# A retention layer and two feed-forward layers on one core: GpSimd's arithmetic placed on VectorE, and each attention unit issued in two halves around the two products of a step

## The chip, the core and the metric

The kernel runs on one NeuronCore of a Trainium2 chip. A core has TensorE (in profiles PE, and PEld for its weight loads), VectorE (DVE), ScalarE (ACT), GpSimd (POOL) and SyncE (SP), which issues most DMAs. The metric is the device time of one execution in microseconds. The kernel before takes 620.3 us (median of three runs, 618.93 to 621.04).

## The reference

Three layers follow each other, all in fp32. The first is a retention layer over 2 batches, 8 heads, 768 positions and head size 64; the two others are feed-forward layers over 1536 tokens, 512 wide inside and 2048 hidden.

```
state = gamma[h] * state + k_t v_t^T          # per batch, head, position t
y_t   = scale * q_t state
x     = y, tokens x 512
x     = softplus(x @ w1_in) @ w1_out          # written as max(h,0) + log1p(exp(-|h|))
out   = (h * clip(h + 3, 0, 6) / 6) @ w2_out, h = x @ w2_in
```

The weights arrive as float64, so every weight is turned into fp32 on the chip from its two 32-bit words.

## The kernel before

**Attention units.** Each batch is cut into 6 pieces of 128 positions, a *unit* each, 12 in all (u = 0 to 11). A unit takes all 8 heads. `scores` multiplies transposed k and q (32 small matmuls per unit in all parts together), and VectorE multiplies both halves by a mask-and-decay table into `pt`. `prepare(u + 1)` transposes k and q of the next unit on TensorE, ScalarE copies them out of PSUM, and `decayed` multiplies v by a table into `vs` (VectorE for units 0 and 1, GpSimd for the others). `carry` multiplies q by the running state `bd` into `o`, and `fade` then scales `bd` by a decay (two GpSimd instructions of 64 x 256). `intra` adds `vs` times `pt` to `o`; VectorE scales the sum into `on`, ScalarE rounds it into `x_hi` (fp32r), and GpSimd subtracts to get the rest, `x_lo`. `state` multiplies k by `vs` and VectorE adds the product to `bd`.

**Feed-forward steps.** A step s is one hidden block f of 128 for one chunk of 512 tokens. `gemm1` multiplies the two parts of `w_in` by the two parts of x in 12 matmuls of 512 columns; ScalarE and VectorE turn the sum into g by `g`, `e`, and split it into `hi` (ScalarE) and `lo` (VectorE). `gemm2`, two steps later (LAG = 2), multiplies `hi` and `lo` by the parts of `w_out` in 12 more matmuls and adds them up in four PSUM banks that are held for a whole chunk. Steps 0 to 15 need chunk 0 only, so units 4 to 11 run beside steps 0 to 7.

**Weights.** `fetch` loads the raw words; `convert` makes a weight tile: ScalarE scales the upper words, VectorE makes four operations (`raw` clamp, `w` shift, two more `w` combinations), then the tile is split into two parts, `t[:, 0]` and `t[:, 1]`. For the first 8 tiles ScalarE copies and GpSimd subtracts (line 97); for the others ScalarE writes -w into `t[:, 1]`, a DMA issued by GpSimd adds w to it (line 100), and ScalarE copies `t[:, 0]`. All 32 tiles of layer 1 are converted beside steps 0 to 15.

**PSUM.** There are eight banks; `bank()` hands them out in rotation. While a chunk holds four, the other four serve the units and `gemm1`: seven requests in a unit with its step, so the bank of a request was last used by the one four requests earlier, and a matmul waits until that bank has been read out.

**Order.** Every engine works through its queue in order. Until unit 3 the queues follow the program. From then on (`nc.on = False`) a scheduler sorts the instructions by when it thinks that they can run, with their place in the program as priority. Line 148 starts the loop in which unit u is followed by step s.

All instructions are recorded on line 31 of a helper, so the profile's groups are told apart by tile names.

Of the kernel before, what the change touches and what calls it, by code (L numbers as in the profile page):

```python
# [10 lines left out]
F32 = mybir.dt.float32  # L11
# [3 lines left out]
ALU = mybir.AluOpType  # L15
# [26 lines left out]
def kernel(ctx, tc, q, k, v, w1_in, w1_out, w2_in, w2_out, tq, tk, tc_, tg, out):  # L42
    nc = InOrder(tc)
# [11 lines left out]
    LAG = 2  # L55
# [27 lines left out]
    def convert(m, o, f):  # L83

        raw = raws.pop((m, o, f))
        low, y = raw[:, :, 0], raw[:, :, 1]

        w = cv_p.tile([P, CH], U32, tag="w", name="w")
        nc.scalar.activation(y.bitcast(F32), y.bitcast(F32), AF.Copy, scale=2.0 ** -112)
        nc.vector.tensor_scalar(y.bitcast(F32), y.bitcast(F32), -TOP, TOP, ALU.max, ALU.min)  # L90
        nc.vector.tensor_scalar(w, y, 3, None, ALU.logical_shift_left)
        nc.vector.scalar_tensor_tensor(w, y, 0x80000000, w, ALU.bitwise_and, ALU.bitwise_or)
        nc.vector.scalar_tensor_tensor(w, low, 29, w, ALU.logical_shift_right, ALU.bitwise_or)
        t = (wout_p if o else win_p).tile([P, 2, CH], F32R, tag="w", name="w_parts")
        if done[1] < 2 * EARLY:
            nc.scalar.activation(t[:, 0], w.bitcast(F32), AF.Copy)
            nc.gpsimd.tensor_tensor(t[:, 1], w.bitcast(F32), t[:, 0].bitcast(F32), ALU.subtract)
        else:
            nc.scalar.activation(t[:, 1], w.bitcast(F32), AF.Copy, scale=-1.0)
            nc.gpsimd.dma_start(out=t[:, 1].bitcast(F32), in_=w.bitcast(F32), accum_op=ALU.add)  # L100
            nc.scalar.activation(t[:, 0], w.bitcast(F32), AF.Copy)
        if o:
            w_out_t[m, f] = t
        else:
            w_in_t[m, f] = t.rearrange("p a (k n) -> p a k n", k=KD)
# [40 lines left out]
    with ExitStack() as actx:  # L146
        unit = attention(actx, tc, nc, q, k, v, tq, tk, tc_, tg, x_hi, x_lo, CH, bank, feed, fetch_weights)
        for u in range(CH // P, NU):
            unit(u)
            step(s)  # L150
            s += 1
    while s < n_steps:
        step(s)
# [3 lines left out]
def attention(ctx, tc, nc, q, k, v, tq, tk, tcc, tg, x_hi, x_lo, CH, bank, feed, fetch_weights):  # L157
# [43 lines left out]

    def decayed(u):
        vs = wk.tile([P, H, D], F32, tag="vs" + "0" * (u < START), name="vs", bufs=2)
        (nc.vector if u < 2 else nc.gpsimd).tensor_tensor(
            vs, nat["v", u], tk_sb.rearrange("p (h o) -> p h o", o=1).to_broadcast([P, H, D]), ALU.mult)
        tr["vs", u] = vs

# [12 lines left out]
    def carry(u):  # L220
        b, i = units[u]
        qT = tr["q", u]
        o = ps(NP, C)
        tr["o", u] = o
        if i > 0:
            for p in range(NP):
                nc.tensor.matmul(o[:, p, :], bd[b][:, p, :], qT[:, p, :], start=(p == 0), stop=False, skip_group_check=True)
        fade(u)

    def intra(u):  # L230
        b, i = units[u]
        vs, pt, o = tr["vs", u], tr["pt", u], tr["o", u]
        for h in range(H):
            g = h % 2
            nc.tensor.matmul(o[g * D:(g + 1) * D, h // 2, :], vs[:, h, :], pt[:, g, h // 2, :],
                             start=(i == 0 and h < 2), stop=True, skip_group_check=True)
        c, at = divmod(u * C, CH)
        hi, lo = x_hi[c][:, :, at:at + C], x_lo[c][:, :, at:at + C]
        on = wk.tile([P, NP, C], F32, tag="on" + "0" * (u < START), name="on", bufs=2)
        nc.vector.tensor_tensor(on, o, tq_sb, ALU.mult)  # L240
        nc.scalar.activation(hi, on, AF.Copy)
        nc.gpsimd.tensor_tensor(lo, on, hi.bitcast(F32), ALU.subtract)

    def state(u):
        b, i = units[u]
# [15 lines left out]
    def fade(u):  # L261
        b, i = units[u]
        if i == 0 or i == NCH - 1:
            return
        for j in range(2):
            r = slice(j * D, (j + 1) * D)
            s = bd[b][r, :, r]
            nc.gpsimd.tensor_tensor(s, s, tc_sb[r].rearrange("p (n o) -> p n o", o=1).to_broadcast([D, NP, D]), ALU.mult)

    for t in bd:  # L270
        nc.vector.memset(t, 0.0)
# [15 lines left out]
    def prepare(u):  # L287
        transposed(u, "k")
        transposed(u, "q")
        decayed(u)  # L290
# [18 lines left out]
        fetch(u, "k", "q", "v")  # L309

    def unit(u):
        scores(u)
        if u + 3 < len(units):
            fetch(u + 3, "k", "q", "v")
        if u + 1 < len(units):
            prepare(u + 1)
        carry(u)
        intra(u)
        state(u)

    return unit

# [1 line left out]
def moe(ctx, tc, nc, out, x_hi, x_lo, w_in_t, w_out_t, chunks1, chunks2, NF, KD, DM, CH, LAG, feed, first, bank, release):  # L324
# [71 lines left out]

    n1 = len(chunks1)

    def step(s):
        if s < len(steps):  # L400
            m, c, ci, f = steps[s]
            gemm1(m, c, ci, f)
            if m == 0 and ci == 0:
                feed(first(f))
            if m == 0 and ci == n1 - 1:
                feed(2 * NF + f + 1)
            if m == 1 and ci == 0:
                feed(3 * NF + f + 1)
        if LAG <= s < len(steps):
            gemm2(*steps[s - LAG])  # L410
        if s == len(steps):
            gemm2(*steps[s - LAG], *(f for _, _, _, f in steps[s - LAG + 1:]))

    return step, LAG, len(steps) + 1
# [38 lines left out]
```

## Time and profile before

| | us |
|---|---|
| median of three runs | 620.3 |
| the profiled execution's own time | 619.72 |
| its span | 617.9 |
| TensorE busy | 595.0 |
| VectorE busy | 353.6 |
| ScalarE busy | 277.5 |
| GpSimd busy | 102.2 |

The profiled execution is 0.6 us under the median; 1.8 us of it lie outside the span. Busy time of TensorE counts a matmul from issue to its modelled end and consecutive matmuls overlap, so a row that starts when the row in front is still running means an engine without a pause. An idle time in a row of groups is the engine's idle time just before these instructions, and the arrow names what ended it.

### The profile page before, as it was taken

The page shows a single profiled execution, that of the slowest core. Times are in us where ns is not written, and L with a number is a line of the kernel's source. Part 1 is how long each engine was busy: PE and PEld are TensorE (multiplying, and loading weights), DVE is VectorE, ACT ScalarE, POOL GpSimd, SP SyncE. Part 2 cuts the span into 40 slices and gives each one's busy share as a digit, 9 for nine tenths or more (in the row PEclk, how much of TensorE's full clock was granted, in tenths as well). Part 3 has the DMA queues.
Part 4 walks back from the last instruction along what each step waited for, and adds up shares of the span by engine and source line. Part 5 has one row for each costly group of instructions (what it writes and reads, how often), then busy time and mean ns, then how long its engine had stood idle before and what let it go on. Part 6 is the DMA issues. An engine that isn't in the chain of part 4 may idle for free.

```text
span 617.9 us, 7766 instructions
## 1 busy us (share of the span) xinstructions
PE 595.0 (96%) x2963; PEld 489.4 (79%) x2963; DVE 353.6 (57%) x583; ACT 277.5 (45%) x473; POOL 102.2 (17%) x110
## 2 busy tenths in 40 slices
PE   7988787999999999999999999999999999999997
PEld 6866576788888888888877878888888888888886
DVE  4599999899863433366667799822422222322223
ACT  3354556578653333465556678722222222222220
POOL 1755455432100000011111123200000000000000
PEclk9999899999999999999999999999999999999999
DMA  9998877788810000045567789700100000100001
GB/s 194 232 235 229 207 183 188 175 216 209 198 37 1 0 1 1 0 95 128 136 152 188 162 203 256 148 0 1 53 16 0 2 1 0 69 0 1 0 1 68
DMA packets 69511, 61.60 MB, mean 100 GB/s; under 512 B 40033, under 2 KB 56673, under 8 KB 69473
## 3 DMA queue, kind: packets, MB, share of 16 engines
q1 hardware_dynamic: 61408, 46.42, 26.8%
q0 software_dynamic: 8064, 14.68, 14.4%
q8 instruction: 23, 0.38, 0.3%
q14 instruction: 16, 0.12, 0.1%
HBM read 43.26 MB, written 3.15 MB: 75 GB/s over the span
## 4 chain that ended last, share of the span: by engine, by line
PE 73%; DVE 14%; DMA 5%; issue 4%; ACT 3%; SPq 1%; POOL 0%; DVEq 0%; POOLq 0%; ACTq 0%
PE banks L31 73%; DVE w L31 6%; DMA raw<-in_moe_w_in_dram 3%; DVE raw L31 2%; DVE g L31 1%; DVE pt L31 1%; DVE e L31 1%; DMA q<-in_q_dram 1%; DVE lo L31 1%; DMA w_parts<-w 1%; ACT raw L31 1%; DVE bd L31 1%; ACT e L31 1%; ACT hi L31 1%; SPq L31 1%
## 5 line engine op out<-in xcount | busy, mean ns | idle before, releaser
L31 PE MATMUL banks<-x_hi,w_parts 128*128 128x512 f32 x768 | 254.6, 392 | 0.0
L31 PEld LDWEIGHTS banks<-x_hi,w_parts 128*128 128x128 f32 x768 | 144.7, 189 | 30.9 <-issue 0.7
L31 PE MATMUL banks<-x_lo,w_parts 128*128 128x512 f32 x384 | 150.2, 391 | 0.0
L31 PE MATMUL banks<-hi,w_parts 128*128 128x512 f32 x384 | 126.9, 391 | 5.3 <-ACT w_parts L31 3.0
L31 PE MATMUL banks<-w_parts,hi 128*128 128x512 f32 (+1 forms) x386 | 118.4, 388 | 0.5 <-DVE g L31 0.5
L31 DVE SCALAR_TENSOR_TENSOR g<-e,banks 128x512 f32<-128x512 f32 x48 | 33.0, 688 | 125.2 <-ACT e L31 125.2
L31 DVE TENSOR_TENSOR lo<-g,hi 128x512 fp32r<-128x512 f32 x96 | 67.3, 701 | 48.0 <-ACT hi L31 47.9
L31 DVE SCALAR_TENSOR_TENSOR w<-raw,w 128x512 uint32<-128x512 uint32 x128 | 92.4, 723 | 1.5
L31 POOL DMA_DIRECT2D w_parts<-w x56 | 48.9, 874 | 254.3 <-ACT w_parts L31 101.0
L31 ACT ACTIVATE e<-banks,three 128x512 f32<-128x512 f32 x48 | 32.9, 685 | 127.6 <-PE banks L31 127.6
L31 PEld LDWEIGHTS banks<-hi,w_parts 128*128 128x128 f32 x384 | 71.9, 188 | 21.5 <-ACT w_parts L31 3.3
L31 ACT ACTIVATE hi<-g 128x512 fp32r<-128x512 f32 x96 | 60.5, 631 | 56.5 <-DVE g L31 56.1
L31 ACT ACTIVATE w_parts<-w 128x512 fp32r<-128x512 f32 x120 | 70.2, 624 | 34.7 <-DVE w L31 34.2
L31 PEld LDWEIGHTS banks<-w_parts,hi 128*128 128x128 f32 x386 | 72.3, 188 | 15.9 <-DVE g L31 0.9
L31 PEld LDWEIGHTS banks<-x_lo,w_parts 128*128 128x128 f32 x384 | 72.4, 189 | 15.0 <-issue 0.3
L31 PE MATMUL banks<-lo,w_parts 128*128 128x512 f32 x192 | 75.2, 392 | 0.4 <-DVE lo L31 0.4
L31 PE MATMUL banks<-w_parts,lo 128*128 128x512 f32 (+1 forms) x193 | 74.9, 388 | 0.0
L31 DVE SCALAR_TENSOR_TENSOR e<-g,banks 128x512 f32<-128x512 f32 x48 | 32.8, 684 | 32.5 <-ACT g L31 32.4
L31 ACT ACTIVATE raw<-raw 128x512 f32<-128x512 f32 x64 | 42.5, 670 | 17.1 <-DMA raw<-in_moe_w_in_dram 17.1
L31 ACT ACTIVATE g<-banks 128x512 f32<-128x512 f32 x48 | 28.4, 592 | 42.2 <-PE banks L31 42.0
L31 DVE TENSOR_TENSOR g<-g,e 128x512 f32<-128x512 f32 x48 | 33.6, 700 | 21.8 <-ACT e L31 21.2
L31 ACT ACTIVATE e<-e 128x512 f32<-128x512 f32 x48 | 30.2, 630 | 30.4 <-DVE e L31 30.1
(45 smaller groups left out, 405.7 us busy)
## 6 DMA issues: line engine op xcount, KB each, us to landing
raw<-in_moe_w_in_dram SPq DMA_DIRECT2D x32, 512.0 KB, 4.1
raw<-in_moe_w_out_dram SPq DMA_DIRECT2D x32, 512.0 KB, 4.8
w_parts<-w POOLq DMA_DIRECT2D x56, 256.0 KB, 4.5
q<-in_q_dram SPq DMA_DIRECT2D x12, 256.0 KB, 5.2
v<-in_v_dram SPq DMA_DIRECT2D x12, 256.0 KB, 5.5
k<-in_k_dram SPq DMA_DIRECT2D x11, 256.0 KB, 5.0
out_dram<-ob SPq DMA_DIRECT2D x11, 256.0 KB, 2.0
k<-in_k_dram SPq DMA_DIRECT2D x2, 128.0 KB, 2.4
```

Source lines behind the costliest of these rows:

```text
L31: ins = getattr(self.engine, op)(*args, **kwargs)
```

## The change

Four kinds of instruction that GpSimd executed are issued to VectorE: `vs` of units 2 to 11 (10 instructions), `x_lo` (12), the scaling of `bd` (16), and the subtraction for the first 8 weight tiles (8). GpSimd keeps the accumulating weight DMAs. The function `unit` now returns two functions, `begin` (the scores and the fetches) and `end` (carry, intra, state and, now last, the preparation of the next unit). `step` takes two flags, so that the loop issues: scores, `gemm1` with its weight conversions, the rest of the unit, `gemm2`.

```
-            nc.gpsimd.tensor_tensor(t[:, 1], w.bitcast(F32), t[:, 0].bitcast(F32), ALU.subtract)
+            nc.vector.tensor_tensor(t[:, 1], w.bitcast(F32), t[:, 0].bitcast(F32), ALU.subtract)
...
         for u in range(CH // P, NU):
-            unit(u)
-            step(s)
+            begin, end = unit(u)
+            begin()
+            step(s, True, False)
+            end()
+            step(s, False, True)
             s += 1
...
-        (nc.vector if u < 2 else nc.gpsimd).tensor_tensor(
+        nc.vector.tensor_tensor(
             vs, nat["v", u], tk_sb.rearrange("p (h o) -> p h o", o=1).to_broadcast([P, H, D]), ALU.mult)
...
-        nc.gpsimd.tensor_tensor(lo, on, hi.bitcast(F32), ALU.subtract)
+        nc.vector.tensor_tensor(lo, on, hi.bitcast(F32), ALU.subtract)
...
-            nc.gpsimd.tensor_tensor(s, s, tc_sb[r].rearrange("p (n o) -> p n o", o=1).to_broadcast([D, NP, D]), ALU.mult)
+            nc.vector.tensor_tensor(s, s, tc_sb[r].rearrange("p (n o) -> p n o", o=1).to_broadcast([D, NP, D]), ALU.mult)
...
     def unit(u):
-        scores(u)
-        if u + 3 < len(units):
-            fetch(u + 3, "k", "q", "v")
-        if u + 1 < len(units):
-            prepare(u + 1)
-        carry(u)
-        intra(u)
-        state(u)
+
+        def begin():
+            scores(u)
+            if u + 3 < len(units):
+                fetch(u + 3, "k", "q", "v")
+
+        def end():
+            carry(u)
+            intra(u)
+            state(u)
+            if u + 1 < len(units):
+                prepare(u + 1)
+
+        return begin, end
...
-    def step(s):
-        if s < len(steps):
+    def step(s, one=True, two=True):
+        if one and s < len(steps):
...
-        if LAG <= s < len(steps):
+        if two and LAG <= s < len(steps):
             gemm2(*steps[s - LAG])
-        if s == len(steps):
+        if two and s == len(steps):
```

TensorE's queue at unit 9, before. `qT,kT` are the scores, `ident` the transposes of the next unit, `qT,bd1` the carry, `pt,vs` the products of `intra`, `hi,w_parts` a matmul of `gemm2`. In brackets stands whose result the instruction waits for.

```order
L31 MATMUL banks_80<-qT_871,kT_865 128x128 [waits Activation_49]
L31 MATMUL banks_80<-qT_871,kT_865 128x128 [waits DVE_49]
L31 MATMUL banks_80<-qT_871,kT_865 128x128 x6
L31 MATMUL banks_80<-ident_101,k_742 128x128 [waits DMAHW0_49,DVE_49]
L31 MATMUL banks_80<-ident_101,k_742 128x128 x3
L31 MATMUL banks_80<-ident_101,q_744 128x128 [waits DMAHW6_49,DVE_49]
L31 MATMUL banks_80<-ident_101,q_744 128x128 x3
L31 MATMUL banks_80<-hi_804,w_parts_816 128x512 [waits Activation_49]
L31 MATMUL banks_80<-qT_871,bd1_113 128x128 [waits DVE_49]
L31 MATMUL banks_80<-qT_871,bd1_113 128x128 x3
L31 MATMUL banks_80<-pt_957,vs_873 64x128 [waits Pool_49]
L31 MATMUL banks_80<-pt_957,vs_873 64x128 [waits DVE_49]
```

The same place with the change, beginning with the last matmul ahead of the scores.

```order
L31 MATMUL banks_80<-lo_767,w_parts_778 128x512
L31 MATMUL banks_80<-qT_941,kT_935 128x128 [waits DVE_49,Activation_49]
L31 MATMUL banks_80<-qT_941,kT_935 128x128 x2
L31 MATMUL banks_80<-qT_941,kT_935 128x128 [waits DVE_49]
L31 MATMUL banks_80<-qT_941,kT_935 128x128 x4
L31 MATMUL banks_80<-qT_941,bd1_113 128x128 x4
L31 MATMUL banks_80<-pt_957,vs_943 64x128 [waits DVE_49]
L31 MATMUL banks_80<-vs_943,k_635 128x128
L31 MATMUL banks_80<-pt_957,vs_943 64x128 [waits DVE_49]
L31 MATMUL banks_80<-pt_957,vs_943 64x128 x6
L31 MATMUL banks_80<-vs_943,k_635 128x128 x3
L31 MATMUL banks_80<-ident_101,k_742 128x128 [waits DMAHW2_49]
```

The transposes have moved behind the unit's other products. The carry has no wait of its own left; both halves of the scores wait for VectorE (their banks were those of `o` and of the state's product in the unit before).

VectorE's queue before, from the `pt` products of unit 9 to the state's update behind them; `raw` and `w` belong to weight conversions, `on` is the unit's scaled sum, `bd1` the running state.

```order
L31 TENSOR_TENSOR pt_957<-banks_80,tm_sb_108 128x512 [waits PE_49] x2
L31 SCALAR_TENSOR_TENSOR w_935<-raw_921,w_935 128x512 [waits DVE_49]
L31 TENSOR_SCALAR raw_933<-raw_933 128x512 [waits DMAHW6_49,Activation_49]
L31 SCALAR_TENSOR_TENSOR w_935<-raw_921,w_935 128x512 [waits DVE_49]
L31 TENSOR_SCALAR w_1030<-raw_933 128x512 [waits DMASW2_49,DVE_49]
L31 TENSOR_TENSOR on_996<-banks_80,tq_sb_106 128x512 [waits PE_49,Pool_49]
L31 SCALAR_TENSOR_TENSOR w_1030<-raw_933,w_1030 128x512 [waits DVE_49]
L31 TENSOR_TENSOR bd1_113<-bd1_113,banks_80 64x4x64 [waits PE_49,Pool_49]
L31 TENSOR_TENSOR bd1_113<-bd1_113,banks_80 64x4x64 [waits Pool_49]
L31 TENSOR_SCALAR raw_1028<-raw_1028 128x512 [waits DMAHW0_49,Activation_49]
```

With the change, from the scaling of unit 8's state (by the table `tc_sb`) to just behind the `pt` products of unit 9.

```order
L31 TENSOR_TENSOR bd1_113<-bd1_113,tc_sb_111 64x4x64 [waits PE_49]
L31 SCALAR_TENSOR_TENSOR w_897<-raw_883,w_897 128x512 [waits DVE_49]
L31 TENSOR_TENSOR bd1_113<-bd1_113,tc_sb_111 64x4x64
L31 TENSOR_TENSOR on_921<-banks_80,tq_sb_106 128x512 [waits PE_49]
L31 TENSOR_TENSOR bd1_113<-bd1_113,banks_80 64x4x64 [waits DVE_49,PE_49]
L31 TENSOR_TENSOR bd1_113<-bd1_113,banks_80 64x4x64 [waits DVE_49]
L31 TENSOR_TENSOR x_lo2_64<-on_921,x_hi2_61 128x4x128 [waits DMAHW2_49,Activation_49]
L31 TENSOR_TENSOR vs_943<-v_639,tk_sb_110 128x512 [waits DMAHW2_49]
L31 TENSOR_TENSOR pt_957<-banks_80,tm_sb_108 128x512 [waits PE_49] x2
L31 SCALAR_TENSOR_TENSOR e_980<-g_981,banks_80 128x512
```

The scaling of `bd`, `x_lo` and `vs` now stand in VectorE's queue; `x_lo` waits there for ScalarE's rounding, and what stood behind `pt` (the scaled sum and the state's update) stands ahead of the next `pt`.

## Rows read from the trace of the kernel before

**Rows 1.** The page: busy time of each engine over the whole span, and VectorE's row of the 40 equal slices (15.4 us each; a digit is the busy share in tenths).

```profile
PE 595.0 (96%) x2963; PEld 489.4 (79%) x2963; DVE 353.6 (57%) x583; ACT 277.5 (45%) x473; POOL 102.2 (17%) x110
DVE  4599999899863433366667799822422222322223
```

**Rows 2.** The table by stretches: length in us, then busy time and (instructions) of PE, PEld, DVE, ACT and POOL, then the granted TensorE clock, the DMA share and GB/s.

```profile
28.90:120.10 91.20, 76.98 (x534) 61.08 (x532) 86.27 (x135) 52.21 (x93) 49.08 (x44) 0.96 0.82 203
120.10:162.00 41.90, 41.45 (x192) 33.74 (x191) 39.90 (x75) 32.33 (x58) 11.94 (x13) 1.00 0.86 211
...
200.00:250.00 50.00, 50.00 (x223) 41.40 (x222) 18.66 (x27) 17.01 (x28) 0.00 (x0) 1.00 0.00 1
```

**Rows 3.** Groups by form in 0 to 125 us, three of TensorE's and ScalarE's: shapes and count, then busy time, mean ns of one, then the idle time of the engine just before them and what ended it.

```profile
L31 PE MATMUL banks<-hi,w_parts 128*128 128x512 f32 x42 | 14.5, 404 | 5.2 <-ACT w_parts L31 3.0 <-POOL w_parts L31 2.2
L31 ACT ACTIVATE w_parts<-w 128x512 fp32r<-128x512 f32 x32 | 19.0, 625 | 22.5 <-DVE w L31 22.2
L31 PE MATMUL banks<-qT,bd 128*128 128x128 f32 x80 | 11.4, 287 | 5.5 <-DVE pt L31 5.5
```

**Rows 4.** Groups by form on VectorE (DVE) in 28 to 121 us, columns as in the group before.

```profile
L31 DVE SCALAR_TENSOR_TENSOR w<-raw,w 128x512 uint32<-128x512 uint32 x39 | 30.2, 777 | 0.2
L31 DVE TENSOR_SCALAR raw<-raw 128x512 f32<-128x512 f32 x20 | 15.0, 751 | 0.1
L31 DVE TENSOR_SCALAR w<-raw 128x512 uint32<-128x512 uint32 x20 | 13.6, 682 | 0.2
L31 DVE TENSOR_TENSOR lo<-g,hi 128x512 fp32r<-128x512 f32 x7 | 5.9, 838 | 0.0
L31 DVE TENSOR_TENSOR g<-g,e 128x512 f32<-128x512 f32 x7 | 5.2, 748 | 0.0
L31 DVE TENSOR_TENSOR bd<-bd,banks 64x256 f32<-64x256 f32 x12 | 5.0, 416 | 1.4 <-PE banks L31 1.1 <-POOL bd L31 0.2
L31 DVE TENSOR_TENSOR on<-banks,tq_sb 128x512 f32<-128x512 f32 x7 | 4.8, 686 | 1.5 <-PE banks L31 1.5
L31 DVE SCALAR_TENSOR_TENSOR e<-g,banks 128x512 f32<-128x512 f32 x7 | 4.8, 684 | 1.8 <-ACT g L31 1.7
```

**Rows 5.** The same groups where GpSimd (POOL) runs no arithmetic: 128 to 176 us (three rows), and 176 to 617 us (last row).

```profile
L31 DVE SCALAR_TENSOR_TENSOR w<-raw,w 128x512 uint32<-128x512 uint32 x26 | 17.9, 687 | 0.3
L31 DVE TENSOR_SCALAR raw<-raw 128x512 f32<-128x512 f32 x15 | 6.4, 424 | 2.7 <-ACT raw L31 2.7
L31 DVE TENSOR_SCALAR w<-raw 128x512 uint32<-128x512 uint32 x12 | 5.1, 421 | 0.0
...
L31 DVE TENSOR_TENSOR lo<-g,hi 128x512 fp32r<-128x512 f32 x80 | 55.3, 691 | 47.3 <-ACT hi L31 47.2
```

**Rows 6.** Instructions of VectorE in order of time: start us, duration us.

```profile
132.46 0.69 DVE L31 SCALAR_TENSOR_TENSOR w<-raw,w 128x512 uint32<-128x512 uint32 x1
133.06 0.42 DVE L31 TENSOR_SCALAR w<-raw 128x512 uint32<-128x512 uint32 x1
133.40 0.69 DVE L31 TENSOR_TENSOR g<-g,e 128x512 f32<-128x512 f32 x1
```

**Rows 7.** Groups by form on GpSimd in 28 to 121 us.

```profile
L31 POOL TENSOR_TENSOR x_lo<-on,x_hi 128x512 fp32r<-128x512 f32 x8 | 11.8, 1472 | 0.5 <-ACT x_hi L31 0.5
L31 POOL TENSOR_TENSOR w_parts<-w,w_parts 128x512 fp32r<-128x512 f32 x8 | 11.4, 1429 | 17.3 <-ACT w_parts L31 17.3
L31 POOL DMA_DIRECT2D w_parts<-w x11 | 9.8, 887 | 15.4 <-ACT w_parts L31 15.4
L31 POOL TENSOR_TENSOR bd<-bd,tc_sb 64x256 f32<-64x256 f32 x10 | 9.5, 952 | 7.8 <-PE banks L31 7.5
L31 POOL TENSOR_TENSOR vs<-v,tk_sb 128x512 f32<-128x512 f32 x7 | 8.3, 1181 | 1.1 <-DMA v<-in_v_dram 0.9
```

**Rows 8.** The same moment in the timelines of GpSimd (first row) and VectorE (second row).

```profile
46.44 1.46 POOL L31 TENSOR_TENSOR x_lo<-on,x_hi 128x512 fp32r<-128x512 f32 x1
...
46.69 1.49 DVE L31 TENSOR_SCALAR raw<-raw 128x512 f32<-128x512 f32 x1
```

**Rows 9.** VectorE's two copies of the `vs` product (units 0 and 1), by form in 0 to 125 us.

```profile
L31 DVE TENSOR_TENSOR vs<-v,tk_sb 128x512 f32<-128x512 f32 x2 | 1.4, 692 | 3.1 <-DMA v<-in_v_dram 3.1
```

**Rows 10.** Marks in the timelines: VectorE at the end of unit 3, at the first weight conversion and at the masked scores of unit 11, then TensorE behind these.

```profile
26.92 0.69 DVE L31 TENSOR_TENSOR on<-banks,tq_sb 128x512 f32<-128x512 f32 x1 [1.72 <-issue]
28.05 0.87 DVE L31 TENSOR_TENSOR bd<-bd,banks 64x256 f32<-64x256 f32 x2 [0.43 <-PE banks L31]
28.95 0.43 DVE L31 TENSOR_SCALAR raw<-raw 128x512 f32<-128x512 f32 x1
120.05 1.28 DVE L31 TENSOR_TENSOR pt<-banks,tm_sb 128x512 f32<-128x512 f32 x2
...
120.88 0.40 PE L31 MATMUL banks<-pt,vs 128*64 128x128 f32 x2 [0.46 <-DVE pt L31]
```

**Rows 11.** Part 6 of the page, the accumulating weight DMAs: count, KB, median us from issue to landing.

```profile
w_parts<-w POOLq DMA_DIRECT2D x56, 256.0 KB, 4.5
```

**Rows 12.** Two stretches of 2 us, in and behind one stop of TensorE (columns as in Rows 2), and one line of the list of waits in 120 to 620 us (us in total, times, longest).

```profile
62.00:64.00 2.00, 0.00 (x0) 0.00 (x0) 2.00 (x5) 0.00 (x0) 0.25 (x1) 1.00 1.04 205
68.00:70.00 2.00, 2.00 (x6) 1.57 (x5) 2.00 (x3) 1.55 (x3) 0.98 (x1) 0.50 1.09 317
...
ACT raw L31 <- DMA raw<-in_moe_w_in_dram: 15.0, 11, 1.9
```

## The prediction

> **What bounds the kernel now.** I read the busy shares first, then the table by stretches, then the groups by form of the stretch that stands out. The page says 96% for TensorE, which tells little, since a matmul counts until its modelled end; VectorE is at nine tenths or near it from the third slice to the eleventh [rows 1]. The stretches say more [rows 2]. In 28.9 to 120.1 us TensorE is busy for 77.0 of 91.2 us and VectorE for 86.3; from 120.1 on TensorE has no pause worth the name (41.45 of 41.9). Where nothing waits, 223 matmuls start in 50 us; two of them reach over an end, so one takes 0.226 us. So VectorE sets the pace until unit 11's masked scores (120.05 us), TensorE runs unbroken behind them from 120.88 [rows 10], and what can be won or lost lies ahead of that mark. TensorE's idle time there stands before the carry (5.5 us, waiting for `pt`, whose bank it reuses) and before the second product (5.2 us, waiting for weight parts) [rows 3].
>
> **VectorE's time before.** Consecutive instructions start 0.60 us apart after one of 0.69 and 0.34 apart after one of 0.42 [rows 6], so each hides about 0.08 under the next: a full operation (128 x 512) occupies 0.61 us, a tensor-scalar one 0.345, a 64 x 256 one 0.34. From the first conversion (28.95) to `pt` of unit 11 (120.05) the queue holds 81 full, 40 tensor-scalar and 12 small instructions: 49.4 + 13.8 + 4.1 = 67.3 us, in a stretch of 91.1. The other 23.8 us have three parts. Idle time is 5.2 us (1.4 + 1.5 + 1.8 and crumbs) [rows 4]. The second is stretching: beside a GpSimd operation VectorE's take longer, as where a clamp of 0.42 took 1.49 us until `x_lo` on GpSimd had ended [rows 8]. By the means of the same forms with and without GpSimd's arithmetic [rows 4, 5]: 39 combinations by 0.777 - 0.687 (3.5 us), 20 clamps by 0.751 - 0.424 (6.5), 20 shifts by 0.682 - 0.421 (5.2), 7 `lo` by 0.838 - 0.691 and 7 `g` by 0.748 - 0.691 (1.4): 16.6 us. The rest, 2.0, are short steps between instructions that depend on each other.
>
> **What is added.** In the same stretch GpSimd executed 8 `x_lo`, 8 subtractions for weights, 10 scalings and 7 `vs`, 41 us in all [rows 7]. On VectorE a `vs` takes 0.692 [rows 9], an `x_lo` or a weight subtraction is the shape of `lo` (0.691) [rows 5]; the scaling is not shown there, and its nearest row is the 64 x 256 update (0.416) [rows 4], which I take. Its bounds are 0.34 and, if the broadcast table were read at half pace, 0.61: at most 2.7 us more over 10. The new queue between the same marks has 159 instructions: 7 `vs`, 7 `x_lo`, 8 subtractions, 10 scalings and one `e` more, 7 of conversions fewer. That is 101 full, 36 tensor-scalar and 22 small: 61.6 + 12.4 + 7.5 = 81.5 us, 14.2 more than before. With GpSimd's arithmetic gone the 16.6 us of stretching go, since the page's stretched forms have their plain durations wherever GpSimd only issues DMAs. So the move alone is worth 2.4 us: nearly nothing. The dependent steps grow with the count, to 2.3 us.
>
> **What the order changes.** Seven bank requests a unit rotate over four banks. Before, the carry's bank was that of the first scores, so TensorE stood until `pt`. Now the carry has no wait; the next scores wait instead, for the scaled sum and the state's update, and transposes and the first product fill the time between. Walking through unit 9 with the durations above: from `pt` of unit 8 VectorE has 10.1 us of work to `pt` of unit 9, and TensorE's part of that loop (24 matmuls, 5.4 us, and the unit's small ones, about 5) is as long. VectorE's inputs from TensorE are then ready some microseconds early. So of the 5.2 us of idle time I keep half, 2.5; the bounds are 0 and 5.2.
>
> **The start.** `x_lo` of unit 3 now stands between `on` (ends 27.6) and the state's update (began 28.05) [rows 10]: ScalarE's rounding (0.63, a copy of the same shape) [rows 3], a signal of 0.1 and 0.61 put that update at 28.95, 0.9 later. Units 1 to 3 each add 1.9 us and one such wait to idle time of 1.72 + 0.43 [rows 10]; the overhang of about 0.4 a unit may cost up to 1.0 more. I take the 0.9.
>
> **The sum.** `pt` of unit 11 comes at 28.95 + 0.9 + 81.5 + 2.3 + 2.5 = 116.2, 3.9 us earlier. At that mark TensorE's new queue is further: 82 matmuls of 512 columns between units 7 and 11 against 87, but 80 against 61 between units 4 and 7, so 14 fewer remain, 3.2 us. Conversions, though, are 1.6 tiles behind. From this `pt` VectorE needs 44 full and 22 tensor-scalar instructions (34.4, with dependent steps 35.4) until tile 12 of the first layer's `w_out` is combined, then come ScalarE's copy (0.63), GpSimd's issue (0.89) [rows 7] and the landing (4.5) [rows 11]: 41.4 us. TensorE would be there after the masked score (0.7), the small products (1.1) and 165 matmuls (37.3): 39.1. It waits 2.3 us in all. Net: 3.9 + 3.2 - 2.3 = 4.8 us. Behind that tile only one conversion a step is left, the queue's lead grows again, and to the end the same matmuls follow at 0.226; nothing later changes. The profiled execution took 619.72 (span 617.9), so 614.9; it was 0.6 under the median, so I say **615.5 us**.
>
> The page "SBUF — State Buffer" of the Trainium skill, section "Who interferes with whom", says that a DMA issued by GpSimd can stall on its descriptors while VectorE runs a two-port operation. A denser VectorE queue would by that rule stretch the accumulating DMAs; one clamp (0.42 us) on each latency would make the sum 4.4. The trace speaks against it so far: the issue takes 0.887 us in the busiest stretch [rows 7].
>
> **Rivals.**
> VectorE waits for ScalarE (slower). The 8 weight subtractions and 7 `x_lo` need a ScalarE copy made moments before, and now hold up VectorE's whole queue; on GpSimd such a wait stood for 17.3 us ahead of 8 [rows 7], and cost nobody. Price by the nearest row: `lo`, which waits for the same kind of copy, idles 47.3 us over 80 late in the kernel, 0.59 each [rows 5], but 0.0 over 7 in the busy stretch [rows 4]. At 0.59 for all 15: 8.9 us, and 624.4 us. It decides from 0.32 us a wait on. Against it: about 0.7 us of other work stands between producer and waiter, as much as the copy takes, and ScalarE is busy for only 52 of 91 us [rows 2].
>
> TensorE's clock falls. Behind the stop of 62 to 64 us it was granted 0.50, its level of 1.2 GHz, in 68 to 70 [rows 12]. Between units 4 and 7 the new queue leaves TensorE short of work in several gaps of 2 to 3 us. Two microseconds at half pace lose 1 us; a stop that costs two such stretches 2 us, three stops 6, if TensorE were on the path: 621.5. VectorE is, so most is hidden; I take 2.5 to 4 us as what could show, 618 to 619.5. The page "TensorE: Matmul & The Clock Gate", section "HAM oscillation — how this bites in real kernels", has just this pattern of short work and gaps; the row agrees with it.
>
> Weights come late. Raw tiles made ScalarE wait 15.0 us in 11 places behind 120 us, 1.4 each [rows 12], and the DMA engines were busy for 0.82 to 0.86 [rows 2] at the old pace. Four such waits, one for each of the units 8 to 11, cost 5.5: 621.0, no change.
>
> VectorE without a pause. Idle time 0 instead of 2.5 and scalings at 0.34: 612.9.
>
> **How the numbers follow.** The forecast has 0.60: its own range is 611.5 to 619, of which 0.57 is faster. VectorE without a pause 0.08, all faster. The clock 0.10 (0.02 faster, 0.08 the same), late weights 0.08 (0.05 the same, 0.03 slower), waits for ScalarE 0.14 (0.03 the same, 0.11 slower), and 0.03 of the forecast is the same. Together faster 0.67, same 0.19, slower 0.14, with 0.3% or 1.9 us as what can be told from no change. The range from 611.5 to 621.5 leaves out most of the waits for ScalarE and a little below.
>
> **What would show it.** Right: clamps at 0.42 and combinations at 0.69 on VectorE ahead of 120 us; `pt` of unit 11 near 116; no idle time before the carry; TensorE unbroken until about 150, then some pauses before second products, waiting for the accumulating DMA, about 2 us together. Wrong: idle time on VectorE before `x_lo` or the weight subtraction, put down to ScalarE, of over 5 us; a granted clock of 0.5 between 35 and 70 for longer than before with late `pt`; ScalarE waiting for raw tiles ahead of 116 us. If stretched forms remain, it was not GpSimd's arithmetic that stretched them.

## The result and the profile after

The changed kernel takes 629.0 us (median of four runs, 626.75 to 630.45) against 620.1 for the kernel before: a ratio of 1.0146, 95% interval 1.0128 to 1.0164. It is slower by 1.5%, and lies outside the predicted range of 611.5 to 621.5. The profiled execution took 627.86 us, its span 626.1.

From the page, busy times and VectorE's row of slices (15.7 us each here) [rows 1]:

```profile
PE 602.8 (96%) x2963; PEld 493.7 (79%) x2963; DVE 359.8 (57%) x629; ACT 277.6 (44%) x473; POOL 49.9 (8%) x64
DVE  4899789998865333366667799932332222422223
```

Stretches of the kernel after (columns as in [rows 2]): from its first conversion to unit 11's masked scores, from there to 188 us, and to 500.

```profile
31.90:123.90 92.00, 82.07 (x539) 65.15 (x540) 83.49 (x161) 51.45 (x91) 8.82 (x10) 0.98 0.75 187
123.90:188.00 64.10, 59.33 (x262) 47.26 (x261) 53.08 (x100) 42.05 (x75) 12.20 (x14) 0.97 0.74 177
188.00:500.00 312.00, 310.96 (x1367) 255.95 (x1366) 166.44 (x279) 145.25 (x250) 27.84 (x32) 1.00 0.32 76
```

The kernel before, the last two of these stretches:

```profile
120.10:188.00 67.90, 67.44 (x307) 55.28 (x306) 57.08 (x104) 46.85 (x83) 12.80 (x14) 1.00 0.65 161
188.00:500.00 312.00, 311.01 (x1368) 256.10 (x1367) 162.89 (x273) 142.02 (x242) 27.86 (x32) 1.00 0.32 76
```

From 188 to 500 us both do the same amount of work, and behind 500 the changed kernel has 35 matmuls more left (541 against 506); so the 8.2 us of difference between the spans arise ahead of 188. Behind unit 11's masked scores TensorE used to be without a pause (67.44 of 67.90); now it stands for 4.8 of 64.1 us.

Groups by form on VectorE in 31 to 124 us [rows 4 and 5]:

```profile
L31 DVE SCALAR_TENSOR_TENSOR w<-raw,w 128x512 uint32<-128x512 uint32 x36 | 24.2, 683 | 0.0
L31 DVE TENSOR_TENSOR pt<-banks,tm_sb 128x512 f32<-128x512 f32 x15 | 10.0, 686 | 4.2 <-PE banks L31 4.0
...
L31 DVE TENSOR_SCALAR raw<-raw 128x512 f32<-128x512 f32 x18 | 7.3, 423 | 0.1
L31 DVE TENSOR_TENSOR x_lo<-on,x_hi 128x512 fp32r<-128x512 f32 x8 | 5.5, 689 | 0.8 <-ACT x_hi L31 0.7
L31 DVE TENSOR_TENSOR w_parts<-w,w_parts 128x512 fp32r<-128x512 f32 x8 | 5.5, 685 | 0.0
...
L31 DVE TENSOR_TENSOR lo<-g,hi 128x512 fp32r<-128x512 f32 x7 | 4.8, 689 | 3.5 <-ACT hi L31 3.5
...
L31 DVE TENSOR_TENSOR bd<-bd,tc_sb 64x256 f32<-64x256 f32 x10 | 4.2, 417 | 0.2
```

The stretching is gone, as forecast: clamps 0.423 instead of 0.751 us, combinations 0.683 instead of 0.777. The moved instructions have the durations that the sum took. `x_lo` waits 0.8 us in all, 0.70 of it in unit 3 ahead of the first conversion, and the weight subtraction not at all. New are 4.0 us ahead of one `pt`, for TensorE, and 3.5 ahead of `lo`.

The marks of [rows 10] in VectorE's timeline (start, duration): units 2 and 3, the first conversion, the two halves of unit 7's `pt`, the longest wait of a `lo`, and unit 11's `pt`.

```profile
23.52 0.69 DVE L31 TENSOR_TENSOR on<-banks,tq_sb 128x512 f32<-128x512 f32 x1
24.91 0.69 DVE L31 TENSOR_TENSOR x_lo<-on,x_hi 128x512 fp32r<-128x512 f32 x1 [0.70 <-ACT x_hi L31]
...
29.11 0.69 DVE L31 TENSOR_TENSOR on<-banks,tq_sb 128x512 f32<-128x512 f32 x1
30.50 0.69 DVE L31 TENSOR_TENSOR x_lo<-on,x_hi 128x512 fp32r<-128x512 f32 x1 [0.70 <-ACT x_hi L31]
...
31.98 0.43 DVE L31 TENSOR_SCALAR raw<-raw 128x512 f32<-128x512 f32 x1
...
73.35 0.69 DVE L31 TENSOR_TENSOR pt<-banks,tm_sb 128x512 f32<-128x512 f32 x1
78.07 0.69 DVE L31 TENSOR_TENSOR pt<-banks,tm_sb 128x512 f32<-128x512 f32 x1 [4.03 <-PE banks L31]
84.41 0.69 DVE L31 TENSOR_TENSOR lo<-g,hi 128x512 fp32r<-128x512 f32 x1 [1.91 <-ACT hi L31]
...
123.83 1.28 DVE L31 TENSOR_TENSOR pt<-banks,tm_sb 128x512 f32<-128x512 f32 x2
```

A unit at the start takes 5.59 us (29.11 - 23.52), and the first conversion comes 3.0 us later than before. The two halves of unit 7's `pt` stand 4.7 us apart. TensorE's timeline shows why (and GpSimd's, last row):

```profile
70.08 1.16 PE L31 MATMUL banks<-qT,kT 64*128 64x128 f32 x8 [1.35 <-DVE on L31]
...
76.45 0.49 PE L31 MATMUL banks<-hi,w_parts 128*128 128x512 f32 x1 [3.39 <-DMA w_parts<-w]
76.88 1.16 PE L31 MATMUL banks<-qT,kT 64*128 64x128 f32 x8
...
70.08 1.02 POOL L31 DMA_DIRECT2D w_parts<-w  x1 [68.43 <-ACT w_parts L31]
```

Between the two halves of the scores stands a piece of a second product: that of step 2, the first whose weight tile has its second part from an accumulating DMA. The DMA was issued at 70.08 and the matmul could start at 76.45. Behind it in TensorE's queue waited the other half of the scores, for it VectorE, and behind `pt` in VectorE's queue the next conversions. In the program this product comes after the scores of unit 8; the scheduler had put a part of it one unit earlier. TensorE's queue there, its lines numbered (w_parts_671 is the tile, `qT_715` belongs to unit 7):

```
104 L31 MATMUL banks_80<-qT_715,kT_709 128x128 x4
105 L31 MATMUL banks_80<-hi_659,w_parts_671 128x512
...
111 L31 MATMUL banks_80<-hi_659,w_parts_671 128x512 x2
112 L31 MATMUL banks_80<-qT_715,kT_709 128x128 x4
```

The granted clock behind this stop, two stretches of 2 us, then 8 us around a later one (columns as in [rows 12]); under them the two later stops of TensorE:

```profile
78.00:80.00 2.00, 2.00 (x11) 1.77 (x10) 1.93 (x5) 0.55 (x1) 0.00 (x0) 0.50 0.64 137
80.00:82.00 2.00, 2.00 (x20) 1.83 (x20) 2.00 (x6) 0.08 (x1) 0.00 (x0) 0.67 0.00 0
168.00:176.00 8.00, 6.61 (x22) 5.29 (x23) 3.73 (x7) 2.61 (x5) 0.89 (x1) 0.79 0.65 142
```

```profile
143.77 0.74 PE L31 MATMUL banks<-hi,w_parts 128*128 128x512 f32 x2 [1.52 <-DMA w_parts<-w]
169.39 0.50 PE L31 MATMUL banks<-hi,w_parts 128*128 128x512 f32 x1 [3.25 <-DMA w_parts<-w]
```

The first stop cost 3.4 us and then 2 x 0.50 + 2 x 0.33 = 1.7 us of clock: in the first of these two stretches TensorE was granted 0.50, its 1.2 GHz level.

### The profile page after: what moved, and what is told of

It is laid out like the page before. It is cut to its first block, busy times and chain, and to the rows that moved or that the text cites. A ratio compares the mean times of both kernels' runs of the same rounds, so it can differ in the third digit from the quotient of the medians.

```text
span 626.1 us, 7701 instructions
## 1 busy us (share of the span) xinstructions
PE 602.8 (96%) x2963; PEld 493.7 (79%) x2963; DVE 359.8 (57%) x629; ACT 277.6 (44%) x473; POOL 49.9 (8%) x64
## 4 chain that ended last, share of the span: by engine, by line
PE 68%; issue 16%; DMA 7%; DVE 6%; ACT 2%; POOL 1%; DVEq 0%; POOLq 0%; ACTq 0%
PE banks L31 68%; DMA raw<-in_moe_w_in_dram 4%; DMA w_parts<-w 3%; DVE w L31 2%; DVE raw L31 1%; POOL w_parts L31 1%; DVE g L31 1%; DVE e L31 1%; ACT raw L31 1%; ACT e L31 1%; ACT hi L31 1%; DVE lo L31 1%; ACT w_parts L31 0%; DVE x_lo L31 0%; ACT g L31 0%
## 5 line engine op out<-in xcount | busy, mean ns | idle before, releaser
L31 PE MATMUL banks<-hi,w_parts 128*128 128x512 f32 x384 | 130.2, 397 | 11.2 <-DMA w_parts<-w 8.2
L31 DVE SCALAR_TENSOR_TENSOR w<-raw,w 128x512 uint32<-128x512 uint32 x128 | 87.3, 686 | 1.4
```

The costliest lines, as they stand in the source:

```text
L31: ins = getattr(self.engine, op)(*args, **kwargs)
```

## The experiments

All times are medians; the ratio, worked out from all runs, is to the kernel before on the same chip, with its 95% interval. The kernel before has medians of 619.2 to 620.1 on the chips used, so differences between medians of different chips are good to about a microsecond.

| run | us | ratio |
|---|---|---|
| changed kernel | 629.0 | 1.0146 [1.0128, 1.0164] |
| e1 move only | 622.8 | 1.0053 [1.0032, 1.0073] |
| e2 order only | 616.7 | 0.9947 [0.9930, 0.9964] |
| e3 start back | 626.2 | 1.0102 [1.0087, 1.0117] |
| e4 12 subtractions | 626.8 | 1.0108 [1.0092, 1.0123] |
| e5 LAG 3 | 634.5 | 1.0235 [1.0219, 1.0250] |
| e6 order only, LAG 3 | 638.5 | 1.0294 [1.0271, 1.0317] |
| e7 less on VectorE | 617.7 | 0.9962 [0.9948, 0.9976] |
| e8 before, LAG 3 | 624.7 | 1.0074 [1.0059, 1.0089] |
| e9 x_lo back | 614.5 | 0.9931 [0.9911, 0.9951] |
| e10 subtractions back | 622.3 | 1.0060 [1.0037, 1.0083] |
| e11 vs, scaling back | 622.9 | 1.0059 [1.0036, 1.0081] |
| e12 fixed order | 617.9 | 0.9991 [0.9974, 1.0009] |
| e13 fixed at one place | 617.5 | 0.9955 [0.9942, 0.9967] |
| e14 fixed, start back | 618.2 | 0.9968 [0.9957, 0.9978] |
| e15 fixed, x_lo back | 616.2 | 0.9942 [0.9921, 0.9963] |
| e16 fixed, 12 subtractions | 621.7 | 1.0029 [1.0016, 1.0041] |
| e17 one DMA left out | 624.0 | 1.0074 [1.0045, 1.0103] |
| e18 the next DMA left out | 629.6 | 1.0164 [1.0137, 1.0191] |

**Halves of the change (e1, e2).** e1 is the kernel before with the four `nc.gpsimd` lines on `nc.vector`; e2 the kernel after with them on `nc.gpsimd` as before.

> The kernel before with the four kinds of GpSimd instruction on VectorE, in the old order of units and steps. Theory (the loss has two places: units 0 to 3, where x_lo waits for ScalarE in VectorE's queue, and later waits of TensorE's queue for accumulating DMAs because conversions stand behind in the new order): the start costs 2 to 3 us as in the changed kernel, GpSimd's stretching goes (2.4 us back), conversions keep their old lead, so hardly a DMA wait: 619 to 622 us. Rival one, the new order alone is the loss: 619 us or less, TensorE without DMA waits. Rival two, the move alone is the loss (VectorE has too much to do): 626 us or more, with pt of unit 11 later than 123.

> The changed order with the arithmetic left on GpSimd. Theory: no loss at the start (first conversion near 29), VectorE stays stretched, conversions are 1.6 tiles behind, so TensorE waits for accumulating DMAs ahead of 180 us for 4 us or more: 623 to 628 us. Rival one, the order is the whole loss: 628 us or more. Rival two, the move is the whole loss: 620 us or less, with DMA waits under 1 us.

e1 came out slightly above the theory's range, e2 below all but the second rival's. Neither part is the loss: the order alone wins, the move alone costs half a per cent, together they cost one and a half. e1 starts its conversions at 31.44, gains the time up to unit 11's `pt` (116.67 us for its first half, where the kernel before had 120.05) and loses it behind, at two waits which the theory had denied it:

```profile
148.56 0.73 PE L31 MATMUL banks<-hi,w_parts 128*128 128x512 f32 x2 [1.19 <-DMA w_parts<-w]
164.26 1.39 PE L31 MATMUL banks<-hi,w_parts 128*128 128x512 f32 x3 [4.05 <-DMA w_parts<-w]
```

**The start (e3)** has `x_lo` and the scaling of units 0 to 3 and `vs` of units 2 and 3 on GpSimd; the first of three like edits:

```
-        nc.vector.tensor_tensor(lo, on, hi.bitcast(F32), ALU.subtract)
+        (nc.gpsimd if u < START else nc.vector).tensor_tensor(lo, on, hi.bitcast(F32), ALU.subtract)
...
```

> The changed kernel, with x_lo, vs and the scaling of the state on GpSimd again for units 0 to 3 alone. Theory: first conversion at 29 to 30 instead of 32, all that follows 2 to 3 us earlier; the waits for accumulating DMAs keep their size, since conversions and products shift together: 626 to 627 us. Rival, the start is hidden behind what TensorE waits for later: 629 us. A second rival, conversions gain more than TensorE does, so the pauses at 144 and 169 shrink too: 622 to 625 us.

626.2: the number fits, the mechanism doesn't. The first conversion is back at 28.95, but TensorE's stop grew to 3.78 us at 76.95 and unit 11's `pt` came at 125.21, later than without the edit.

**Fewer accumulating DMAs (e4)**: `if done[1] < 3 * EARLY`.

> The changed kernel with 12 instead of 8 weight tiles split by subtraction on VectorE, so that the first four accumulating DMAs go (two of them for w_out). Theory (TensorE's queue stands at 76 us for the landing of the first such DMA, amid unit 7's scores): that pause of 3.4 us and VectorE's idle time of 4.0 behind it go, VectorE gets 4 x 0.61 = 2.4 us more work, the clock does not fall at 78: pt of unit 11 2 to 4 us earlier, 625 to 627 us. Rival, only VectorE's load decides: pt of unit 11 2.4 us later, 631 us or more.

626.8, with unit 11's `pt` at 119.89 and no stop at 76: as the theory had it. But TensorE now waited 7.2 us for accumulating DMAs between 124 and 188, where the changed kernel has 4.8.

**Second products one step later (e5, e6, e8)**: `LAG = 3`, and `bufs=4` for hi and lo, in the changed kernel, in e2 and in the kernel before.

> The changed kernel with the second product three steps behind the first instead of two (LAG = 3, and four buffers for hi and lo). No VectorE instruction is added or removed. Theory (the loss is TensorE standing at second products for weight tiles that come late, at 76, 144 and 169 us, with the clock falls behind them): one step more, 5.4 us, covers waits of 3.4, 1.5 and 3.3, so they go: 620 to 623 us, no idle time of TensorE over 1 us put down to the accumulating DMA. Rival (VectorE's total work up to the last tile of layer 1 sets the end, whoever waits where): the last of the 24 accumulating DMAs of layer 1 is still issued near 177 us, other waits take the place of these, 626 us or more.

> The changed order with the arithmetic left on GpSimd (616.7 us) and LAG = 3. It has no waits for accumulating DMAs to lose, so one theory as the other gives 615 to 618 us; below 614 would say that conversions still held TensorE up there.

> The kernel before with LAG = 3, a control for the two kernels above: the kernel before has no wait of TensorE for an accumulating DMA, so 619 to 621 us by either theory. 617 us or less would say that second products were held up by conversions there too.

e6 and e8 missed. e5 is slower than the changed kernel, where its rival said 626 us or more, but that says nothing for the rival. The control shows that LAG = 3 has a cost of its own in 300 to 400 us, where layer 2 begins: TensorE is busy for 94.2 of 100 us in e8 and 92.2 in e5, against 99.0 in the kernel before. And in e5 TensorE still stood 4.04 us at 78.35 for an accumulating DMA, and VectorE 5.8 us for TensorE behind it. So this tells little of the cause.

**Less work for VectorE (e7)**

```
-        nc.vector.tensor_tensor(lo, on, hi.bitcast(F32), ALU.subtract)
+        if u < START:
+            nc.vector.tensor_tensor(lo, on, hi.bitcast(F32), ALU.subtract)
...
-        if i == 0 or i == NCH - 1:
+        if i == 0 or i == NCH - 1 or u >= START:
             return
...
```

> The changed kernel with x_lo left out for units 4 to 11 (the buffers hold zeros) and the scaling of the state left out from unit 4 on: 8 x 0.61 + 10 x 0.34 = 8.3 us less on VectorE, and nothing else moved to another engine. Theory that VectorE's total work up to the last tile of layer 1 sets the end: the last accumulating DMA of layer 1 is issued about 8 us earlier (near 170), 621 to 624 us. Rival (the place of the second products in TensorE's queue and the landing of the DMAs set it): the pause at 76 us stays, and the time falls by 2 us or less, 627 us or more.

617.7, below both ranges: 11.3 us for 8.3 us of work. TensorE's queue had changed too: between the halves of unit 7's scores stood only three matmuls, with the part of the tile that ScalarE writes, and TensorE waited for no accumulating DMA at all. The run does not tell load and order apart.

**One kind back (e9 to e11)**: one of the moved kinds on GpSimd again.

> The changed kernel with x_lo alone on GpSimd again (all 12). Theory (VectorE's load up to the last tile of layer 1 is the path; an operation on GpSimd costs VectorE 0.40 us of stretching for each of its own): a 1.47 us x_lo costs VectorE 0.59 instead of 0.61, so only the start (3.0 us) comes back: 625 to 627 us. Rival (x_lo's and lo's waits for ScalarE and the stops that follow are the loss, not the load): 621 us or less.

> The changed kernel with the subtraction for the first 8 weight tiles alone on GpSimd again. By load: 8 x (0.61 - 0.57) = 0.3 us, 628 to 629.5 us. Rival (these subtractions hold up the conversions behind them, and so the tile that TensorE stands for at 76): that stop shrinks or goes, 625 us or less.

> The changed kernel with vs of units 2 to 11 and the scaling of the state on GpSimd again. By load: 8 x (0.61 - 0.47) less 12 x (0.38 - 0.34) = 0.6 us: 628 to 629.5 us. Rival (these 0.34 and 0.61 us operations, which have their operands early, fill VectorE's queue ahead of conversions; on GpSimd they cost next to nothing): 625 us or less.

All three gain far more than the load theory allows (6 us where it gives 0.5, 14 where it gives 3), and that sinks it as the main cause. e9 beats both kernels and has the lowest time of all, though the intervals of e2, e13 and e15 overlap with its own. In e9 the scheduler left unit 7's scores whole, and TensorE waits for no accumulating DMA at all; e10 has four shorter waits, 4.0 us together, in an execution of 625.8 us, its slowest; e11 kept a stop of 4.46 us and gained 6 us all the same, so that stop is not the whole loss.

**The order on TensorE (e12, e13).** A function `pin` keeps the scores and second products of layer 1's first chunk in program order (e12: units 4 to 11 and blocks 0 to 5; e13: units 7 and 8 and block 2 alone). No instruction is added, removed or put on another engine. e13:

```
...
+                if u in (7, 8):
+                    pin(nc, mm)
...
+                        if m == 0 and ci == 0 and f == 2:
+                            pin(nc, mm)
```

> The changed kernel, with the scores of units 4 to 11 and the first six second products held in the order of the program on TensorE, so that the second product with the first accumulated tile stands behind unit 8's scores instead of amid unit 7's. VectorE's instructions are the same. Theory: TensorE's stop of 3.4 us at 76 and VectorE's idle time of 4.0 behind it go, VectorE gains those 4 us up to the last tile of layer 1: 624 to 626 us. Rival (the idle time turns up at another wait of VectorE): 628 us or more.

> The changed kernel with the order of the program kept on TensorE at one place alone: the scores of units 7 and 8 and the second product of step 2 (the first that needs an accumulated tile). Theory that the one stop of TensorE at 76 us is the loss, and that all later waits follow from it: 617 to 620 us, no wait of TensorE for an accumulating DMA over 1 us, the last accumulating DMA of layer 1 issued near 164. Rival (second products stand too early in several places, unit 7's is one of them): 623 us or more, and other stops remain.

Both go further than the theory had said of e12, and e13 lies in the range that it gives for the one place: 617.5 us, 11.5 less than the changed kernel. e13's waits of TensorE in 28 to 200 us hold no accumulating DMA:

```profile
PE banks L31 <- ACT w_parts L31: 4.2, 4, 1.4
PE banks L31 <- DVE bd L31: 2.4, 2, 2.1
PE banks L31 <- DVE on L31: 1.4, 1, 1.4
PE banks L31 <- ACT qT L31: 0.3, 1, 0.3
PE banks L31 <- ACT kT L31: 0.3, 1, 0.3
```

VectorE's two halves of unit 7's `pt` stand together again, unit 11's comes at 117.28, and the last accumulating DMA of layer 1 is issued at 164.37, not at 177.67. From unit 11's `pt` to that issue TensorE runs unbroken and at full clock:

```profile
117.28 1.29 DVE L31 TENSOR_TENSOR pt<-banks,tm_sb 128x512 f32<-128x512 f32 x2
```

```profile
117.28:164.37 47.09, 47.09 (x224) 39.01 (x223) 45.65 (x86) 36.44 (x65) 11.38 (x13) 1.00 0.86 203
```

**The start, x_lo and the load under the fixed order (e14 to e16)**: e12 with the edits of e3 (`x_lo` alone), e9 and e4.

> The kernel with the scores and the first six second products in program order (617.9 us), and x_lo of units 0 to 3 on GpSimd. If the start's 3.0 us are on the path, as they look once the stop is gone: first conversion near 29, 614 to 616 us. If TensorE waits for something else later: 617 to 618 us.

> The same with all of x_lo on GpSimd. By load (0.59 us of stretching against 0.61) the x_lo of units 4 to 11 are neutral: the same as with those of units 0 to 3 alone, 614 to 616 us. If x_lo's waits for ScalarE in VectorE's queue cost something in these units too: 613 us or less.

> The kernel with the scores and the first six second products in program order, and 12 weight tiles by subtraction instead of 8: 4 x 0.61 = 2.4 us more on VectorE, four accumulating DMAs less. If VectorE's load up to the last tile of layer 1 is the path: 619 to 621 us. If the landing of the accumulating DMAs still holds TensorE up: 617 us or less. If, as without the fixed order, TensorE still comes to wait late for accumulating DMAs: 625 us or more.

e14 is 618.2 where e12 is 617.9 (by the ratios it gains 1.4 us, with intervals that overlap): most of the start's 3.0 us are given back, VectorE waiting 3.3 us for one `lo` at 68.29. e15, 616.2, lies just above what was expected; it is 2.0 us under e14, though by load it should be the same, and what gives that is open. e16, 621.7, lies 0.7 above the range of the load theory and fits it better than the other two: 2.4 us more on VectorE, and its ratio is 0.38% above e12's, 2.4 us. And some 5 us of e4's time were its order, not its subtractions (626.8 against 621.7).

**The stop alone (e17, e18).** e13 also moved other instructions behind unit 7. e17 keeps the changed kernel's order on every engine (but for two neighbouring matmuls) and leaves out the one DMA; e18 leaves out the next.

```
-            nc.gpsimd.dma_start(out=t[:, 1].bitcast(F32), in_=w.bitcast(F32), accum_op=ALU.add)
+            if done[1] != 8:
+                nc.gpsimd.dma_start(out=t[:, 1].bitcast(F32), in_=w.bitcast(F32), accum_op=ALU.add)
```

> The changed kernel without one DMA: the accumulating DMA of weight tile 8 (of w_out, block 2) is left out, so that its second part stays -w. The instructions of VectorE, ScalarE and SyncE stand in the same order as in the changed kernel, and TensorE's too but for two neighbouring matmuls. Theory (the landing of this one DMA stops TensorE amid unit 7's scores, and all of the loss follows from it): no stop at 76, VectorE's idle time of 4.0 goes, pt of unit 11 near 117 to 118, 617 to 621 us. Rival (the order from unit 7 on is what costs, the stop is a part of it): only the stop's own 3.4 to 4 us go, 625 us or more.

> The control: the changed kernel without the accumulating DMA of weight tile 9 (of w_in, block 6), for which TensorE did not wait. If it matters which DMA goes, 628 to 630 us, with the stop at 76 us as before; if less DMA traffic alone helps, 625 us or less.

The control is as slow as the changed kernel. e17 lies between the two theories: 624.0, so the stop with its clock fall and what follows from it is worth 5.0 of the 11.5 us (5.6 against the control, on the same chip). The same 10 us in the changed kernel (first row) and in e17 (second):

```profile
72.00:82.00 10.00, 6.61 (x41) 5.32 (x40) 5.90 (x13) 2.48 (x5) 0.86 (x1) 0.83 0.77 178
```

```profile
72.00:82.00 10.00, 9.99 (x69) 8.16 (x69) 9.21 (x18) 5.43 (x10) 1.02 (x1) 1.00 0.64 165
```

The other 6.5 us lie in the order from unit 7 on, ahead of which e13's queues of TensorE and VectorE are the changed kernel's. e17's stops of TensorE and its clock there:

```profile
132.33 0.73 PE L31 MATMUL banks<-hi,w_parts 128*128 128x512 f32 x2 [0.50 <-DMA w_parts<-w]
138.80 0.72 PE L31 MATMUL banks<-hi,w_parts 128*128 128x512 f32 x2 [0.74 <-DMA w_parts<-w]
150.22 0.73 PE L31 MATMUL banks<-hi,w_parts 128*128 128x512 f32 x2 [0.22 <-DMA w_parts<-w]
165.00 0.70 PE L31 MATMUL banks<-hi,w_parts 128*128 128x512 f32 x1 [3.37 <-DMA w_parts<-w]
```

```profile
156.00:172.00 16.00, 12.63 (x49) 9.93 (x49) 10.54 (x19) 9.05 (x17) 2.60 (x3) 0.89 0.74 166
```

At unit 11's `pt` (119.14) e17 has started 160 large matmuls since 28 us, as many as the changed kernel at its own (512 columns; 64 + 43 + 32 + 21 in its groups by form); e13 has 146 at 117.28. The changed order's TensorE is 14 matmuls ahead there. But its last accumulating DMA goes out at 173.28, 8.9 us after e13's, and TensorE waits 4.8 us and loses 16 x 0.11 = 1.8 at the lower clock: what was ahead is waited away.

The traces show how a late tile makes the next ones late. The stretch from unit 11's `pt` to that last issue in e17, and under it ScalarE and VectorE behind its stop that ended at 165.00:

```profile
119.14:173.28 54.14, 49.31 (x216) 38.73 (x215) 45.47 (x86) 36.71 (x65) 11.32 (x14) 0.97 0.77 180
```

```profile
168.95 0.63 ACT L31 ACTIVATE hi<-g 128x512 fp32r<-128x512 f32 x1 [3.47 <-PE banks L31]
169.62 0.69 DVE L31 TENSOR_TENSOR lo<-g,hi 128x512 fp32r<-128x512 f32 x1 [3.65 <-ACT hi L31]
```

VectorE does the same 86 instructions as in e13, 45.5 against 45.7 us, but in 54.1 instead of 47.1 us. Where TensorE stood for a DMA, ScalarE's next `hi` waited for that second product, VectorE's `lo` for `hi`, and the conversions behind `lo` came later still. Over all profiled executions with LAG = 2 the span follows the issue of layer 1's last accumulating DMA: 160.7 to 165.3 goes with 612.5 to 618.0 us, 169.1 to 173.3 with 620.0 to 621.4, and 175.9 to 179.8 with 624.0 to 627.4. Which of the moved instructions brings the first tiles late is open.

## Why the prediction was wrong

**Stretching, durations, the move's work: right.** The sum gave VectorE 81.5 us and 2.3 of dependent steps between the two marks. Measured: 91.85 us from 31.98 to 123.83, of which VectorE was busy for 83.4 (83.49 of the 92.00 us of the first stretch above) and idle for 8.5. The scaling took 0.417, the duration of the update by whose row it was sized; the sum had it at the 0.34 that this row occupies, which the rival without a pause lists as a gain once more.

**The start: mis-sized.** 3.0 us instead of 0.9, and beyond the bound of 1.9. `on` of unit 3 started at 29.11 instead of 26.92: units 0 to 2 lost 2.2 us ahead of the place that was counted, since `x_lo` waits 0.70 us in each and VectorE has hardly any other idle time there. Unit 0, which was not counted, cost 1.25 of it (`on` of unit 1 at 17.93 instead of 16.68); units 1 and 2 cost 0.47 each, the overhang that was left at nothing. The signal of 0.1 in that sum has no row beside it; the 0.70 holds the copy of 0.63 and 0.07 for both signals. By e14 most of the start does not reach the end.

**The step that failed is the idle time.** "VectorE's inputs from TensorE are then ready some microseconds early. So of the 5.2 us of idle time I keep half" was worked out by walking through unit 9, and taken for all units. At unit 7 TensorE's queue holds a second product between the two halves of the scores, and its tile arrives 6.4 us after GpSimd's issue. Idle time was 8.5 instead of 2.5 us, 4.03 + 1.91 of it right behind that stop. With the start (2.1 more) and the work (83.8 forecast, 83.4 measured) that is 6.0 + 2.1 - 0.4 = 7.7: unit 11's `pt` came at 123.83, not at 116.2. With the program's order kept at that one place (e13) it came at 117.28.

**The tail: a false gain.** The forecast booked 14 matmuls that TensorE is further as 3.2 us won, and set 2.3 against them for late tiles. The lead is there (160 against 148 started by the records, some missing), but it was work brought forward at the conversions' expense: the waits were 1.52 + 3.25, and the clock of 0.79 in 168 to 176 took 8 x 0.21 = 1.7 more, 6.5 us where 2.3 were forecast. That a late tile delays `hi`, `lo` and so the next tiles was not in the sum. With the lead at 12 matmuls (2.7 us) the stretch up to `pt` and the tail explain 7.7 + 4.2 + 0.5 = 12.4 of the 13.0 us by which the profiled execution missed its 614.9. e13, without that lead, has neither wait nor clock fall there.

**The rivals.** VectorE waiting for ScalarE ahead of the 15 new instructions, the main one on the slower side, did not happen: 0.8 and 0.0 us from 31 to 124. The clock fell, but behind stops, as a part of their price; the Trainium skill's page "TensorE: Matmul & The Clock Gate", section "HAM oscillation — how this bites in real kernels", has this pattern of gaps and slow work, and 0.50 behind the stop of 3.39 us agrees. Raw weight tiles made ScalarE wait twice between 28 and 124 us, 3.7 us together, under the 5.5 that this rival needed. A DMA's landing in the middle of TensorE's queue was among none of the rivals, although `hi,w_parts` waiting for weight parts stood in [rows 3] and the landing of 4.5 us in [rows 11].

The carry has 0.3 us of idle time left, of 5.5, as forecast. The forecast number itself, 615.5, is within 2 us of what e13 takes with the same instructions on the same engines, but not by the forecast's terms: e13 has neither the lead of 14 matmuls nor the late tiles.

## What to carry to other kernels

Read the new queue of the bounding engines for every unit of the stretch, not for one, and ask at each instruction that needs a DMA what stands behind it; here the scheduler put one ahead of work that was urgent. An engine that gets further in the same time has gained only if what it needs next is also earlier. When moves of single parts all gain more than their work, suspect the order that they change, and take away the wait alone with the order kept.

## What the runs showed of the hardware

The accumulating DMA that stopped TensorE took 6.4 us from issue to use, where the median of landings was 4.5 us before [rows 11] and 4.8 after. GpSimd's issue of such a DMA took 0.876 us (24 in 31 to 188 us) where VectorE executed more instructions (161 in 92.0 us instead of 135 in 91.2), against 0.887 [rows 7]; the stall of which the Trainium skill's "SBUF — State Buffer", section "Who interferes with whom", speaks does not show in this issue time. VectorE's busy share was no higher, though (0.91 against 0.95), so this is a mild test. In e2, where GpSimd kept its arithmetic, combinations on VectorE took 0.887 us, more than the 0.777 before, in an execution (619.8 us, the slowest of ten) as fast as the kernel before (619.7): how much VectorE is stretched said little of the time.
